# Two transformer layers: quarters of product rounds beside the scores, masked Q by DMA, V copies on GpSimd

## The chip, the cores and the metric

The kernel runs on one core of one Trainium2 chip. The core has five engines that run their own instruction streams and meet through semaphores: TensorE (PE; its weight loads are listed as PEld), VectorE (DVE), ScalarE (ACT), GpSimd (POOL) and SyncE (SP), which here only issues DMAs. The metric is the device time of one execution in microseconds.

## The reference

One sequence of 2048 rows and width 512 passes twice through an attention layer and an MLP, with the same weights both times:

```python
def _A_ref(x, wqkv, wo):                    # H = 32 heads of Dh = 16
    qkv = (x @ wqkv).reshape(B, S, 3, H, Dh).transpose(2, 0, 3, 1, 4)
    q, k, v = qkv[0], qkv[1], qkv[2]
    p = softmax(einsum("bhqd,bhkd->bhqk", q, k) * Dh ** -0.5)
    return einsum("bhqk,bhkd->bhqd", p, v).transpose(0, 2, 1, 3).reshape(B, S, D) @ wo
def _B_ref(x, w1, b1, w2, b2):              # F = 1792
    return gelu(x @ w1 + b1) @ w2 + b2
x = x + _A_ref(layernorm(x));  x = x + _B_ref(layernorm(x))
x = x + _A_ref(layernorm(x));  x = x + _B_ref(layernorm(x))
```

## The kernel before, in words

**Cells.** The attention is cut into cells. A cell is one head, one tile of 128 keys and one chunk of 512 queries: 2 layers x 32 heads x 16 key tiles x 4 chunks = 4096 cells. K and Q are stored transposed, four groups of two heads deep in the partitions: a strip `a` of 32 partitions holds two heads of 16. A *pass* takes one chunk of queries and four heads, one out of each strip, over its key tiles (16, which makes 64 cells, or fewer in the passes that are cut in two); eight passes cover the 32 heads. The last chunk of layer 1 goes in two halves of 256 queries, with both heads of a strip in one cell. To take one head of the two in a strip, the kernel makes a copy of Q, `QP`, in which the rows of the other head are zero; there are two slots of it, used by turns.

**Scores.** `score` is one matmul of 32 rows by 128 columns (the strip's 32 rows, 128 keys), which streams 512 queries into a PSUM bank. Matmuls on different strips run side by side. `scores` issues a group of two cells for ScalarE, and may add a third (`more`) or cells for VectorE (`attach`, `trade`). A run of such matmuls in one tiling is called a score stretch here. `solo` issues a VectorE cell alone.

**Exponentials.** ScalarE takes two or three cells with one Exp activation over neighbouring banks (`exps`, the profile's L2234). VectorE takes single cells (`dfirst`, L1867): one multiply-add whose integer result is read as a bfloat16, a coarse exponential. Two further copies of that tile with a constant added (`shift`, L2097, on GpSimd; or L2099 on VectorE) and products with V scaled by two weights make it precise. So a VectorE cell needs three products with V (plain V once, the scaled copies `VC` twice) where a ScalarE cell needs one. `KD` names the key tiles that may go to VectorE; `vcopies` (L1526) makes `VC`.

**Products.** `pvs` collects ready tiles into rounds: four matmuls of 128 rows (keys) by 17 columns (16 of V and a column of ones for the sum), one for each strip's head, side by side in the four column strips of one PSUM bank, number 6 (`PVB`, the only one). After the last round of a pass `norm` reads the bank.

**Rest.** Projections, output projection and the two MLP matmuls run as 128x32 tiles (`quads`, L715). Where PE would idle, `fill` lets it run matmuls whose result is not used (L1586).

**Order.** All of it is laid out before the launch by a planner (`_Plan` on `_Sched`): each job is a thread that yields operations with a cost, keys that it reads and writes, and a priority; the scheduler picks the operation that can start first by its own clock of each engine, and writes each engine's instructions in that order, with the semaphore waits that the keys demand. The engines then run their lists in order. The planner counts a change between the tilings "S" (scores) and "P" (rounds) with `SW` on PE. `ROWS` holds sets of rule values, and `PIECES` says which set holds in which part of the kernel. `_Op.apart` are matmuls issued behind an operation at no counted cost.

Of the kernel before, what the change touches and what calls it, by code (L numbers as in the profile page):

```python
# [5 lines left out]
ALU = mybir.AluOpType  # L6
# [9 lines left out]
H = 32  # L16
# [9 lines left out]
PT_RING = 30  # L26
# [37 lines left out]
KWAIT = (140, 230, 320)  # L64
KSTEP = 10
QSTEP = 10
KLAST = 1
NKD = 7
# [27 lines left out]
         "CLOSE",)  # L96
ROWS = (
# [42 lines left out]
)  # L140
PIECES = (4, 23, 28, 27, 28, 25, 25, 25, 23, 25, 20, 25, 25, 25, 20, 20, 20, 24, 15, 36, 36, 30, 31, 24, 24, 24, 33, 33, 24, 24, 24, 0, 0,
          5, 5, 37, 25, 25, 6, 25, 14, 18, 30, 30, 3, 35, 37, 5, 19, 19, 5, 20, 38, 41, 38, 35, 35, 35, 35, 24, 17, 17, 17, 14, 19, 7, 7, 7,
          18, 18, 18, 39, 39, 22, 15, 1, 41, 41, 39, 41, 39, 25, 25, 2, 2, 14, 23, 25, 25, 35, 35, 32, 32, 34, 36, 32, 38, 41, 41, 32)
# [53 lines left out]
class _Prog:  # L197
# [77 lines left out]
    def group(self, eng, fns, reads=(), writes=(), sem=None, by=1):  # L275
        if sem is None:
            sem = ENG_SEM[eng]
        self._dep_waits(eng, reads, writes)
        for i, fn in enumerate(fns):
            last = i == len(fns) - 1  # L280
            self.prog[eng].append(("do", fn, sem if last else None, by if last else 0))
# [423 lines left out]
class _Plan:  # L705
# [801 lines left out]
    def vcopies(self):  # L1507
# [4 lines left out]
        for v in range(len(first)):  # L1512
# [17 lines left out]
            if not js:  # L1530
                continue
# [890 lines left out]
```

## Time and profile before

| | |
|---|---|
| median of 3 runs | 1375.13 us (1374.58 to 1377.1) |
| profiled execution | 1374.89 us |
| its span, first to last instruction | 1373.1 us |
| granted TensorE clock | 1.0 |

The page gives busy times and groups of instructions; a group's row has its count, busy us, mean ns of one, and the idle time of its engine just before it with what ended it. Matmuls overlap and their ends are modelled, so PE's use is better read from starts in the timeline. The windows view gives busy us of each engine within a stretch, with the granted clock, the DMA engines' share and GB/s.

### The profile page before, as it was taken

The page shows a single profiled execution, that of the slowest core. Times are in us where ns is not written, and L with a number is a line of the kernel's source. Part 1 is how long each engine was busy: PE and PEld are TensorE (multiplying, and loading weights), DVE is VectorE, ACT ScalarE, POOL GpSimd, SP SyncE. Part 2 cuts the span into 40 slices and gives each one's busy share as a digit, 9 for nine tenths or more (in the row PEclk, how much of TensorE's full clock was granted, in tenths as well). Part 3 has the DMA queues.
Part 4 walks back from the last instruction along what each step waited for, and adds up shares of the span by engine and source line. Part 5 has one row for each costly group of instructions (what it writes and reads, how often), then busy time and mean ns, then how long its engine had stood idle before and what let it go on. Part 6 is the DMA issues. An engine that isn't in the chain of part 4 may idle for free.

```text
span 1373.1 us, 42332 instructions
## 1 busy us (share of the span) xinstructions
PE 1338.8 (98%) x18168; PEld 390.1 (28%) x18168; DVE 1261.8 (92%) x2504; ACT 1349.0 (98%) x1385; POOL 802.8 (58%) x1352
## 2 busy tenths in 40 slices
PE   9999999999999999999999999999999999999999
PEld 3222222222222222222222222222222222333446
DVE  8999999989999899998979899999999898999894
ACT  7999999999999999999999999999999999999995
POOL 1367667657665567665626666546656665765461
DMA  5300000123221221112451141100104314201112
GB/s 149 72 2 1 2 2 23 49 75 97 71 43 45 89 83 55 44 51 65 114 109 40 49 128 57 48 17 12 37 24 117 93 40 143 83 14 44 29 34 83
DMA packets 122296, 80.20 MB, mean 58 GB/s; under 512 B 36732, under 2 KB 121084, under 8 KB 122108
## 3 DMA queue, kind: packets, MB, share of 16 engines
q1 hardware_dynamic: 122108, 77.49, 20.6%
q8 instruction: 143, 2.34, 0.7%
q14 instruction: 45, 0.37, 0.1%
HBM read 65.67 MB, written 4.19 MB: 51 GB/s over the span
## 4 chain that ended last, share of the span: by engine, by line
ACT 83%; PE 10%; DVE 6%; DMA 1%; issue 0%
ACT pt L2234 70%; PE ps L715 5%; ACT kt L2234 3%; ACT g L1276 3%; PE ps L1598 3%; ACT v L2234 2%; PE ps L2301 2%; DVE dp L1867 2%; ACT q L2234 2%; DVE kt L1867 1%; ACT L2234 1%; ACT L1276 1%; ACT g L2234 1%; DVE stats L848 0%; DMA wr<-in_B_w_dram 0%; DMA wr<-in_A_wqkv_dram 0%
## 5 line engine op out<-in xcount | busy, mean ns | idle before, releaser
L2234 ACT ACTIVATE pt<-ps 128x1024 bf16<-128x1024 f32 (+1 forms) x1183 | 1142.7, 1176 | 2.0 <-PE ps L1598 1.6
L1598 PE MATMUL ps<-qp,kt 32*128 32x512 bf16 x4096 | 551.5, 384 | 16.6 <-ACT pt L2234 12.2
L2097 POOL INT64_ADD dp<-dp x732 | 440.2, 613 | 204.8 <-DVE dp L1867 123.1
L1867 DVE TENSOR_SCALAR dp<-ps 128x512 uint16<-128x512 f32 x733 | 483.3, 679 | 26.3 <-PE ps L1598 23.4
L1598 PEld LDWEIGHTS ps<-qp,kt 32*128 32x128 bf16 x4096 | 138.4, 91 | 569.7 <-ACT pt L2234 466.7
L2097 POOL INT64_ADD kt<-kt x320 | 190.1, 599 | 174.1 <-DVE kt L1867 93.6
L2301 PE MATMUL ps<-pt,v 128*17 128x512 bf16 (+1 forms) x2758 | 273.9, 359 | 1.4 <-ACT pt L2234 0.7
L1867 DVE TENSOR_SCALAR kt<-ps 128x512 uint16<-128x512 f32 x309 | 207.4, 683 | 23.4 <-PE ps L1598 20.8
L2301 PE MATMUL ps<-dp,vc 128*17 128x512 bf16 (+1 forms) x1652 | 220.7, 357 | 0.6 <-POOL xf L2097 0.4
L2301 PE MATMUL ps<-dp,v 128*17 128x512 bf16 (+1 forms) x826 | 139.1, 357 | 3.4 <-DVE xt L1076 2.4
L2097 POOL INT64_ADD v<-v x155 | 94.1, 611 | 71.7 <-DVE v L1867 35.8
L715 PE MATMUL ps<-xf,wr 128*32 128x512 bf16 (+1 forms) x1888 | 134.6, 366 | 0.5 <-DVE g L1258 0.4
L2301 PE MATMUL ps<-kt,vc 128*17 128x512 bf16 (+1 forms) x766 | 117.6, 340 | 1.0 <-POOL xf L2097 0.3
L1867 DVE TENSOR_SCALAR v<-ps 128x512 uint16<-128x512 f32 x154 | 102.8, 682 | 13.2 <-PE ps L1598 12.8
L715 PE MATMUL ps<-wr,g 128*32 128x512 bf16 x1408 | 108.1, 384 | 0.5 <-DVE dp L1867 0.2
L2301 PEld LDWEIGHTS ps<-pt,v 128*17 128x17 bf16 x2758 | 69.8, 88 | 74.5 <-issue 51.8
L2301 PE MATMUL ps<-kt,v 128*17 128x512 bf16 (+1 forms) x507 | 85.8, 350 | 1.7 <-DVE xt L1076 1.0
L2097 POOL INT64_ADD xf<-xf x78 | 46.5, 596 | 65.5 <-DVE xf L1867 40.3
L1258 DVE TENSOR_SCALAR g<-ps,hb1t 128x512 bf16<-128x512 f32 (+1 forms) x112 | 78.9, 706 | 1.0 <-PE ps L715 1.0
L2301 PEld LDWEIGHTS ps<-dp,vc 128*17 128x17 bf16 x1652 | 56.7, 88 | 42.0 <-issue 24.4
L2234 ACT ACTIVATE kt<-ps 128x1024 bf16<-128x1024 f32 (+1 forms) x60 | 63.4, 1189 | 0.0
L2301 PE MATMUL ps<-v,vc 128*17 128x512 bf16 x308 | 60.8, 381 | 0.0
(124 smaller groups left out, 1425.5 us busy)
## 6 DMA issues: line engine op xcount, KB each, us to landing
wr<-in_B_w_dram SPq DMA_DIRECT2D x174, 256.0 KB, 2.9
wr<-in_A_wqkv_dram SPq DMA_DIRECT2D x24, 256.0 KB, 3.3
x<-in_A_x_dram SPq DMA_DIRECT2D x7, 512.0 KB, 4.3
wr<-in_A_wo_dram SPq DMA_DIRECT2D x10, 256.0 KB, 3.7
kept<-x SPq DMA_DIRECT2D x4, 512.0 KB, 3.1
x<-kept SPq DMA_DIRECT2D x4, 512.0 KB, 4.4
out_dram<-x SPq DMA_DIRECT2D x16, 128.0 KB, 2.5
q<-in_B_w_dram SPq DMA_DIRECT2D x3, 512.0 KB, 4.5
```

Source lines behind the costliest of these rows:

```text
L715: return [lambda e, a=a: e.matmul(out[32 * a:32 * a + 32, :], lhsT=lhsT[:, 32 * a:32 * a + 32], rhs=rhs, start=start, stop=stop, tile_posi ...
L1258: yield _Op("dve", 0.21 + n / 966, lambda e, fc=fc, pb=pb: e.tensor_scalar(T["G"][:, fc, q], pb, T["HB1T"][:, fc:fc + 1], None, op0=ALU.ad ...
L1276: lambda e, g=g: e.activation(out=g, in_=g, func=ACT.Gelu_apprx_tanh), reads=gk, writes=gk, prio=2)
L1598: return (lambda e: e.matmul(o, lhsT=lhsT, rhs=rhs, start=True, stop=True, tile_position=(32 * a, 0)), ["K%d.%d.%d" % (l, gb, kt // 4), "Q ...
L1867: yield _Op("dve", 0.682, lambda e: e.tensor_scalar(u, self.bank(b), E_SCALE, E_BIAS, op0=ALU.mult, op1=ALU.add), reads=["B.%d" % b], writ ...
L2097: op = _Op("pool", PFIX + PWORD * 128 * (hi - lo), lambda e: e.int64_add(dst, src, by * PACKED), reads=reads, writes=writes)
L2234: yield _Op("act", EXPC + 0.4267 * n, lambda e, src=src, dst=dst: e.activation(out=dst, in_=src, func=ACT.Exp, scale=0.25), reads=["B.%d" ...
L2301: op.fns.append(lambda e, o=o, lhsT=q[0][0][m], rhs=q[0][1][:, n * m:n * m + n], a=a, st=st, sp=sp: e.matmul(o, lhsT=lhsT, rhs=rhs, start= ...
```

## The change

- **Quarters** (`beside`, `quarter`, `rest`, `avoid`, `freed`): behind a score stretch that leaves a strip of rows unused, PE also gets a quarter of a product round: the four products restricted to 32 of their 128 rows, as 32x32 tiles in that strip. Four quarters make a round. At most two rounds are open at a time (`PARTS`), at most one quarter goes to a stretch, a new round is opened only while each column of the pass has at least `PLEFT` (4 to 12, mostly 7) key tiles left. Each quarter waits for the one before it. What is left at the end of a pass is issued alone.
- **Wide cells** (`wide`, `solo`): a VectorE cell issued alone may run as a round of four 128-row by 32-column tiles against a copy of Q that is zero outside the head's 16 rows; only for strip 3, and only where that copy was made by DMA. `solo` gets a further condition under which it issues such a cell.
- **Masked Q** (`qpad`): instead of a multiplication by a 0/1 mask on VectorE, five DMAs copy the 16 rows of each strip's head into `QP` (the other rows stay zero) and those of strip 3 into two further slots. This holds for full-width passes that don't follow passes of four key tiles or fewer.
- **V copies** (`vcopies`, `vpart`): on GpSimd, and for the passes that are cut in parts by chunk of keys, so that a part can be used before the others.
- **Space**: `PT_RING` 29, `NKD` 6, `QP` four slots.
- **Order anew**: new rows in `ROWS`, new `PIECES`.

The core of the diff:

```diff
-PT_RING = 30
+PT_RING = 29
+PARTS = 2
+PLEFT = 7
+STEER = 1
+WSOLO = 0.4
+WBACK = 9
+QCOST = 0.6
+QTAIL = 2.2
+VCP = 1.1
-NKD = 7
+NKD = 6
...
-            for f, r, w in op.apart:
+            for f, r, w, *order in op.apart:
+                for x in order:
+                    for y in x:
+                        self.P.wait(e, *y)
                 ev = self.P.group(e, [f], r, w)
+                for x in order:
+                    x[:] = [ev]
...
+    def vpart(self, v, pi, js):
...
+            yield _Op("pool", 0.2 + VCP * len(js) / 6, lambda e, i=i, w=w: e.tensor_scalar(
+                T["VC"][:, v % VCR, i, js[0]:js[-1] + 1, 0:H // 4 * 17], src, w, None, op0=ALU.mult),
...
-            s = yield ("acq", "qp")
+            s = pi % 2
+            yield ("take", ("qp", s))
+            if len(ts) == 1 and ts[0] == s and pi > 1 and min(len(x[3]) for x in self.pas[pi - 2:pi]) > 4:
+                fns = []
+                for a in range(4):
+                    p = slice(32 * a + DH * s, 32 * a + DH * s + DH)
+                    fns.append(lambda e, ...: e.dma_start(T["QP"][p, s, :], T["Q"][p, b, 512 * qc:512 * qc + 512]))
+                p = slice(96 + DH * s, 96 + DH * s + DH)
+                fns.append(lambda e, ...: e.dma_start(T["QP"][p, 2 + s, :], T["Q"][p, b, 512 * qc:512 * qc + 512]))
+                yield _Op("sp", QCOST, fns, ..., sem="dqp%d" % s, by=80, tail=QTAIL)
...
+    def beside(self, op, start, cells):
+        if self.s.mode != "S":
+            self.laid = False
+        cur = self.cur
+        if cur is None or self.laid or not all(cur["begun"]):
+            return
+        idle = [r for r in range(4) if all(c[2] != r for c in cells)]
+        if not idle:
+            return
+        cur["more"] = min(self.pvleft[k] for k in cur["cols"]) >= PLEFT
+        part = next((x for x in cur["parts"] if x["left"] & set(idle)), None)
+        if part is None and cur["more"] and len(cur["parts"]) < PARTS:
...
+        r = next(r for r in idle if r in part["left"])
+        part["left"].discard(r)
+        op.apart.append((self.quarter(cur, part, r, ...), part["keys"], ["B.%d" % cur["b"]], self.order))
+        self.laid = True
...
+    def quarter(self, cur, part, r, end):
+        bank, n = self.bank(cur["b"]), cur["n"]
+        row = slice(32 * r, 32 * r + 32)
+        def f(e):
+            for m in range(512 // n):
+                for a, ws, p in part["work"]:
+                    x = e.matmul(bank[32 * a:32 * a + 17, n * m:n * m + n], lhsT=ws[m][row, :], rhs=p[row, n * m:n * m + n],
+                                 start=False, stop=..., tile_position=(32 * r, 32 * a))
+            return x
+        return f
...
+    def wide(self, cell, qs, bank):
...
+        return (self.quads(self.bank(bank), self.T["K"][l][:, gb, kt * 128:(kt + 1) * 128], self.T["QP"][:, 2 + qs, :], True, True),
+                ["K%d.%d.%d" % (l, gb, kt // 4), "QZ.%d" % qs])
...
+            cur["more"] = False
+            yield ("cond", lambda cur=cur: not cur["parts"] or self.ended or self.s.force or self.s.clock["act"] < self.s.clock["pe"] + 0.3)
+            self.cur = None
+            for i, x in enumerate(cur["parts"]):
+                self.s.force = False
+                for r in sorted(x["left"]):
+                    op = _Op("pe", MM, [self.quarter(...)], reads=x["keys"], writes=["B.%d" % b], prio=0.5, mode="S")
+                    op.late = lambda op, start: self.P.wait("pe", "pe", self.P.cnt["pe"])
+                    yield op
```

More of the change, by code (lines that the diff above doesn't have):

```diff
@@ L64 @@
 KWAIT = (140, 230, 320)
+PARTS = 2
+PLEFT = 7
+PAGE = 10
+STEER = 1
+WSOLO = 0.4
+WBACK = 9
+WSIDE = 0
+QCOST = 0.6
+QTAIL = 2.2
+VCP = 1.1
 KSTEP = 10
@@ L1529, in vcopies @@
-            yield ("give", ("vc", v))
-            if not js:
-                continue
-            self.lend = 1
+            if not kd:
+                continue
+            old = used[v % VCR]
+            if old is not None:
+                yield ("cond", lambda pi=first[old + 1]: self.pv >= pi)
+                for part in self.vparts(first[old]):
+                    yield ("need", ("vc", old, part[-1]))
+            used[v % VCR] = v
+            for part in self.vparts(first[v]):
+                yield ("spawn", self.vpart(v, first[v], part), 4)
@@ L1561, in free @@
         k = "B.%d" % PVB
-        if best[1] > now and (self.pvwas if k in ahead else self.pvopen) and "VC.0.0" in P.lastw:
+        if best[1] > now and (self.pvwas if k in ahead else self.pvopen) and "VC.0.0.0" in P.lastw:
             best = (PVB, 0.0)
@@ L1599, in score, with avoid @@
                 ["K%d.%d.%d" % (l, gb, kt // 4), "QP.%d" % qs] + ["K0.0.0.b"] * ((l, gb) == (0, 0) and kt in (2, 3)))
+    def avoid(self):
+        parts = self.cur["parts"] if self.cur and STEER else []
+        left = set.union(*[x["left"] for x in parts]) if parts else set()
+        return left if parts and (len(parts) == PARTS or not self.cur["more"]) and len(left) < 3 else set()
     def next_act(self, used=()):
+        most = self.avoid() | set(used)
         while self.pa < len(self.pas):
@@ L1604, in next_act @@
                 if q:
-                    return q.pop(next((k for k, c in enumerate(q) if c[2] not in used), 0))
+                    k = next((k for k, c in enumerate(q) if c[2] not in most), None)
+                    return q.pop(next((k for k, c in enumerate(q) if c[2] not in used), 0) if k is None else k)
             self.pa += 1
         return None
-    def next_d(self, used, start, pop=True):
+    def beside(self, op, start, cells):
[10 more added lines that the diff above has]
+        if part is None and cur["more"] and len(cur["parts"]) < PARTS:
+            got = []
+            for k in cur["cols"]:
+                for q in (self.aq[k], self.dq[k]):
+                    i = next((i for i, x in enumerate(q) if ("V", cur["l"], x[5], x[5] // 4) in self.s.tokens and self.s.landed(x[2]) <= start
+                              and not any(y[0] == "seen" for y in x[3])), None)
+                    if i is not None:
+                        got.append((k, q, i))
+                        break
+            if len(got) < 4 or cur["wait"] and not self.rest(got, start):
+                return
+            part = {"left": set(range(4)), "work": [], "keys": [], "back": []}
+            for k, q, i in got:
+                x = q.pop(i)
+                part["work"].append((k[1], x[0], x[1]))
+                part["keys"] += x[2]
+                part["back"] += x[3]
+                self.pvleft[k] -= x[4]
+            cur["parts"].append(part)
+        if part is None:
+            return
+        r = next(r for r in idle if r in part["left"])
+        part["left"].discard(r)
+        op.apart.append((self.quarter(cur, part, r, len(cur["parts"]) == 1 and not part["left"] and not any(self.pvleft[k] for k in cur["cols"])),
+                         part["keys"], ["B.%d" % cur["b"]], self.order))
+        self.laid = True
+        self.units_done += 1
+        if not part["left"]:
+            cur["parts"].remove(part)
+            for pool, x in self.freed(part["back"]):
+                self.s.pools[self.s.route(pool, x)].append(x)
@@ new lines, in rest @@
+    def rest(self, got, start):
+        took = [id(q[i]) for _, q, i in got]
+        for k in self.cur["cols"]:
+            for q in (self.aq[k], self.dq[k]):
+                x = next((x for x in q if id(x) not in took), None)
+                if x is not None and ("V", self.cur["l"], x[5], x[5] // 4) in self.s.tokens and self.s.landed(x[2]) <= start:
+                    return True
+        return False
+    def quarter(self, cur, part, r, end):
[4 more added lines that the diff above has]
+                for a, ws, p in part["work"]:
+                    x = e.matmul(bank[32 * a:32 * a + 17, n * m:n * m + n], lhsT=ws[m][row, :], rhs=p[row, n * m:n * m + n], start=False, stop=end and m == 512 // n - 1,
+                                 tile_position=(32 * r, 32 * a))
+            return x
+        return f
@@ new lines, in freed, with next_d @@
+    def freed(self, back):
+        for pool, r in back:
+            if pool == "seen":
+                r[0]["seen"][r[1]] += 1
+                continue
+            if pool == "du":
+                self.duleft[r] -= 1
+                if self.duleft[r]:
+                    continue
+            if pool == "pl":
+                if not self.drop(*r):
+                    continue
+                r = r[1]
+            yield pool, r
+    def next_d(self, used, start, pop=True, wide=False):
@@ L1650, in join @@
             self.open = None
-        f, r = self.score(d, self.s.tokens[("qp", d[0])], b)
+        f, r = (self.wide if op.mode == "P" else self.score)(d, self.s.tokens[("qp", d[0])], b)
         if op.fns and not self.third(b):
@@ L1656, in join @@
         else:
-            op.fns.append(f)
+            op.fns += f if op.mode == "P" else [f]
             op.reads += r
@@ L1881, in chance @@
                 return self.ended
+            bank = bool(pools["dbank"] or pools["misc"]) and bool(self.open or self.roomy())
+            if bank and s.clock["dve"] <= s.clock["pe"] + WSOLO and s.clock["act"] >= s.clock["pe"] + WBACK:
+                side = sum(th.op.cost for th in s.threads if th.op is not None and th.op.eng == "pe" and th.prio >= 10)
+                if side <= WSIDE and self.next_d((), s.clock["pe"], False, True):
+                    return True
             if s.clock["act"] < s.clock["pe"] + ALONE:
@@ L1893, in solo @@
                 return
-            d = self.next_d((), s.clock["pe"])
+            d = self.next_d((), s.clock["pe"], wide=True)
+            mode = "P" if d else "S"
+            self.wides += mode == "P"
+            d = d or self.next_d((), s.clock["pe"])
             b = (pools["dbank"] or pools["misc"]).pop(0)
-            op = _Op("pe", MM, [], mode="S", prio=1.2)
+            op = _Op("pe", MM, [], mode=mode, prio=1.2)
             extra = []
             self.join(op, d, b, extra)
+            if mode == "S":
+                op.late = lambda op, start, d=d: self.beside(op, start, [d])
             yield op
@@ L2259, in pvs @@
             begun = [False] * 4
+            self.cur = cur = {"b": b, "l": l, "n": n, "cols": cols, "begun": begun, "parts": [], "more": True, "wait": False}
             def have(k):
@@ L2294, in build @@
                     rounds += 1
-                    end = all(self.pvleft[k] == sum(q[0][4] for x, q in got if x == k) for k in cols)
+                    end = not cur["parts"] and all(self.pvleft[k] == sum(q[0][4] for x, q in got if x == k) for k in cols)
                     for m in range(512 // n):
```

96 lines of the change are left out of this document (56 added, 40 removed), and 122 rows, old and new, of the table ROWS.

## The prediction

> **What bounds the kernel now.** I read the page first, then the windows, then a stretch of the timeline in the middle, then groups by line.
>
> ```profile
> span 1373.1 us, 42332 instructions
> PE 1338.8 (98%) x18168; PEld 390.1 (28%) x18168; DVE 1261.8 (92%) x2504; ACT 1349.0 (98%) x1385; POOL 802.8 (58%) x1352
> ACT 83%; PE 10%; DVE 6%; DMA 1%; issue 0%
> ```
> The last line is the chain that ended last: mostly ScalarE's exponentials (L2234). The profiled run took 1374.89 us, 1.8 over its span and 0.24 below the median of the three runs shown, 1375.13; I sum against the span and add 1.8. About 0.2% (2.75 us) is what a measurement can tell from no change.
>
> ```profile
> 13.80:1360.00 1346.20, 1317.13 (x17802) 378.52 (x17806) 1249.42 (x2453) 1338.29 (x1363) 799.89 (x1343) 1.00 0.21 57
> 300.00:400.00 100.00, 99.02 (x1256) 26.22 (x1252) 98.25 (x208) 100.00 (x109) 64.56 (x108) 1.00 0.32 78
> 700.00:800.00 100.00, 97.75 (x1262) 25.65 (x1262) 85.23 (x144) 99.94 (x101) 54.33 (x91) 1.00 0.23 61
> ...
>   PE ps L1598: 63.1, 172
> ```
> Busy us of PE, PEld, DVE, ACT, POOL, then granted clock, DMA share, GB/s. Between the first score and the last layer's end (1346.2 us; 26.9 lie around it) ScalarE idles 7.9 us. Nothing shortens that part unless cells (one score tile of 128 keys by 512 queries) leave ScalarE for VectorE. VectorE is 92.8% busy there, 98% in some stretches and 85% in others; 63.1 us of its idle time before L1867 ends with a score from PE (last line). So three engines stand close together, and a relief must reach all three.
>
> ```profile
> 600.38 0.39 PE L1598 MATMUL ps<-qp,kt 32*128 32x512 bf16 x3
> 600.70 0.40 PE L715 MATMUL ps<-xf,wr 128*32 128x512 bf16 x4
> 600.92 0.39 PE L2301 MATMUL ps<-v,vc 128*17 128x512 bf16 x3
> 601.25 0.39 PE L1598 MATMUL ps<-qp,kt 32*128 32x512 bf16 x3
> 601.57 0.39 PE L2301 MATMUL ps<-pt,v 128*17 128x512 bf16 x1
> 601.58 0.38 PE L2301 MATMUL ps<-v 128*17 128x512 bf16 x1
> ```
> Starts tell PE's true price (ends are modelled). Round to round is 0.22 us; score to round 0.32, round to score 0.33: each change of tiling costs 0.10, and a stretch of scores with both changes 0.43. The four matmuls of a round start within 0.01. The stretches hold three cells: one of four 32-row strips streams nothing.
>
> ```profile
> L2234 ACT ACTIVATE pt<-ps x1183: 1017/1177/1682, 12.2 to 1339.9; 128x1024 bf16<-128x1024 f32 x180, 128x1536 bf16<-128x1536 f32 x18
> L2234 ACT ACTIVATE kt<-ps x60: 1017/1177/1647, 212.1 to 809.7; 128x1024 bf16<-128x1024 f32 x56, 128x1536 bf16<-128x1536 f32 x4
> L2234 ACT ACTIVATE v<-ps x46: 1030/1182/1627, 1003.5 to 1343.8; 128x1024 bf16<-128x1024 f32 x39, 128x1536 bf16<-128x1536 f32 x7
> L2234 ACT ACTIVATE q<-ps x26: 1055/1190/1641, 215.4 to 1178.9; 128x1024 bf16<-128x1024 f32 x23, 128x1536 bf16<-128x1536 f32 x3
> L2234 ACT ACTIVATE g<-ps x8: 1024/1476/1637, 342.6 to 878.9; 128x1536 bf16<-128x1536 f32 x5, 128x1024 bf16<-128x1024 f32 x3
> 1108.48 3.67 ACT q L2234 x4
> L1867 DVE TENSOR_SCALAR dp<-ps x733: 628/680/1137, 37.7 to 1339.8; 128x512 uint16<-128x512 f32 x184
> L1867 DVE TENSOR_SCALAR kt<-ps x309: 627/683/693, 140.0 to 1330.6; 128x512 uint16<-128x512 f32 x155
> L1867 DVE TENSOR_SCALAR v<-ps x154: 645/681/693, 197.9 to 658.3; 128x512 uint16<-128x512 f32 x154
> L1867 DVE TENSOR_SCALAR xf<-ps x77: 652/682/693, 31.7 to 1185.0; 128x512 uint16<-128x512 f32 x77
> L1867 DVE TENSOR_SCALAR xp<-ps x54: 628/680/692, 33.5 to 765.8; 128x512 uint16<-128x512 f32 x54
> ```
> 1323 exponentials, so some 1323 score stretches. The chain spends 3.67 on four of two cells: 0.46 per cell. VectorE has 1327 of the 4096 cells, at 0.68 each.
>
> **1. Quarters in the idle strip.** A round of four 128-row products is cut into four 32-row quarters, each issued behind a score stretch in a strip that it leaves free, at most one per stretch. 4096 cells are 64 passes of 64 cells, with 20.7 stretches each. A new round may start while all columns have 7 of 16 key tiles left, over 9/16 of a pass (11.6); the first products must be begun, and the two rounds open at the end run on: I take 12 per pass, 770 quarters. If they stream beside the scores, each saves a quarter of 0.22 (0.055) and costs four more starts (0.01): 35 us of PE. Upper end: 1300 quarters at 0.055, 71 us. The lower end is below zero, since no row shows 32-column beside 128-column tiles. The nearest:
>
> ```profile
> 1356.28 0.33 PE L902 MATMUL ps<-ident,xln 128*128 128x128 bf16 x3
> 1356.55 0.40 PE L715 MATMUL ps<-q,g 128*32 128x512 bf16 x4
> L902 PE MATMUL ps<-ident,xln x24: 219/219/230, 8.1 to 1356.4; 128*128 128x128 bf16 x24
> ```
> Three transposes in 0.33 with 0.22 each step by 0.055; the third has streamed at 1356.45, and the 128x32 tiles start at 1356.55. Going from 128 to 32 columns alone thus costs 0.10, on shared rows. Against that, score cells on different strips start together. I take the strips as independent, nearest to that row, which is the only one with disjoint rows; the other reading is rival D. By the Trainium skill, TensorEngine Tiling (Array Packing), Key Properties, a change of tiling mode drains the array, and 32x128 and 32x32 are listed as two modes; by that rule each quarter costs two drains and the sum is D's. The trace agrees for shared rows (0.10); no run here shows disjoint ones.
>
> A quarter's buffers stay held for up to four stretches, and PE waits for its own previous quarter: done one round earlier (0.33+0.32 ahead), so nothing. Behind that wait stands all of PE.
>
> **2. Masked Q by DMA; V copies on GpSimd.**
>
> ```profile
> L1545 DVE TENSOR_SCALAR qp<-q,mask 128x512 bf16<-128x512 bf16 x75 | 25.4, 338 | 0.2 <-PE ps L1598 0.2
> L1526 DVE TENSOR_SCALAR vc<-v 128x816 bf16<-128x816 bf16 x60 | 21.1, 357 | 0.0
> L1526 DVE TENSOR_SCALAR vc<-v 128x680 bf16<-128x680 bf16 x10 | 3.4, 370 | 0.0
> L1526 DVE TENSOR_SCALAR vc<-v 128x136 bf16<-128x136 bf16 x18 | 2.9, 188 | 0.0
> L1196 SPq DMA_DIRECT2D wr<-in_B_w_dram x174: 367/368/955, 10.7 to 1348.6; - x174
> x<-in_A_x_dram SPq DMA_DIRECT2D x4, 128.0 KB, 2.3
> SPq L1196 <- PE ps L1598: 535.0, 86, 152.2
> L2097 POOL INT64_ADD dp<-dp x732 | 440.2, 613 | 204.8 <-DVE dp L1867 123.1 <-DVE ott L1085 14.6 <-DVE qp L1545 13.2
> L756 POOL MEMSET v<- 128x512 bf16 x1 | 2.3, 2275 | 0.0
> ```
> Of the 75 full-width masks, 9 follow the first short passes and 11 the short ones of layer 1; 55 go to DMA: 18.6 us off VectorE, and the copies another 27.4: 46.0.
>
> SP pays 55 x 5 issues of 0.37: 1.8 us each, landing 1.8 + 2.3 = 4.1 us after the first (nearest row: 128 KB loads; 2.7 if the issues overlap, 13.4 if all five landings queue up). Hidden, by either bound: a mask's slot frees when the pass two before has been scored, 21 us (1346.2/64) ahead of its use. Not hidden: SP works in order, and its weight loads wait for ring buffers up to 152.2 us; a mask behind such a load is late, and every score of its pass with it. That is rival E; here zero. The mask's wait on SP in turn holds the weight loads behind it, whose ring is four deep: zero.
>
> GpSimd takes 88 copies of up to 816 elements. Its rows give bounds: an add of 0.61 and a memset of 2.28; far apart and neither a copy, so I take their geometric mean, 1.2: 106 us (54 to 200). By the Trainium skill, GPSIMD Engine Reference, Elementwise side-by-side cycle accounting, a light one-input body runs at 1.03 cycles per element, as an estimate 0.70 us at 1.2 GHz for 816 elements, so 62 us; the trace shows no such copy. Behind a pair of copies an add waits 2.4 us, and product rounds behind that. GpSimd goes from 800 us to 800 + 106 + 38 (31 more pairs of cells, two adds of 0.61 each) = 944 of 1318, 72%, and its idle 28% and the other products that PE can take first hide that: zero, and at most 44 x 2.4 = 106 us if nothing did. The zeroing of the extra Q rows, one memset at the start while GpSimd idles: zero. One exponential buffer fewer of 30: no ScalarE wait of the trace ends with PE's products, zero; without that cover it costs ScalarE waits of a round, 0.22.
>
> **3. Lone cells as rounds.** A lone cell costs a stretch of 0.43 now; as 32-column tiles of all 128 rows it costs a round, 0.22. Only strip 3 with a DMA-made mask qualifies, and the new condition for extra ones needs ScalarE 9 us ahead, as around its GELUs. 0 to 100 cells, 0 to 21 us of PE; I take 5.
>
> **4. How much moves (order anew).** Let x cells leave ScalarE and M be the length of the middle. ScalarE: M = 1346.2 - 0.46x. VectorE, busy a share s: 1249.4 - 46.0 + 0.68x = sM. If nothing but its load changes, s = 92.8%, x = 41, M = 1327. If all its waits for scores went, s = 97.5% (63.1/1346.2 more); the best windows have 98%, which gives x = 102, M = 1299. PE decides between them.
>
> ```profile
> L1586 PE MATMUL ps<-b2row 128*32 128x512 bf16 x324 | 26.9, 384 | 0.1
> L1586 PE MATMUL ps<-b2row,zero 128*17 128x512 bf16 x80 | 7.3, 383 | 0.0
> ```
> 101 rounds are fillers, 22 us; without them PE is busy 1295 of 1346.2, 96.2%. With the change: -35 quarters, -5 lone cells; and per moved cell -0.21 (half a stretch), +0.11 (two more products of four to a round), and 1.5 seats, as the cell and half of the one that its stretch carried need one: 0 in a fourth strip, 0.43 alone, 0.21 taken: +0.32. Together 1255 + 0.215x. At the old 96.2% that meets ScalarE's line at x = 61, M = 1318; VectorE then stands at s = 94.5%, between its bounds. Sum: span 1318 + 26.9 = 1345, time **1347** (28 us less, 2.0%). Ends, by s: 1328 (98%) and 1356 (92.8%).
>
> **Rivals.** B, the change does not do what it says: quarters are rare, or eat their gain in held buffers and in left-over quarters that end a pass alone (0.43 each, with a wait for the one before). With no net gain from them PE needs 1290 + 0.215x, which meets ScalarE at x = 8, M = 1343: time 1371. For it: VectorE and PE were both short of slack, so little else moves. Against: an idle strip in almost every stretch. Range 1356 to 1371.
>
> D, slower: the strips are not independent, and a quarter drains the array, as the 0.10 for 128 to 32 columns suggests. Then it streams behind the scores, 0.22 + 0.10 more, in place of 0.055 saved: 770 x 0.32 = 246 us on PE, 1290 + 246 + 13 = 1549 at x = 61, nearly full: about 1590. It decides early: once a quarter adds over 0.01 us net, PE needs 8 us more than in B and the whole is slower than before. Against it: four scores on different strips start within 0.01 and need no common timing.
>
> E, slower: masks late on SP. Scores of a pass then wait with all engines; 0.5 to 1 us in each of 55 passes makes 28 to 55 us: 1375 to 1402. For it: the 535 us of SP waits. Against: 21 us of lead.
>
> **How the numbers follow.** The forecast (1328 to 1356) 0.56, B 0.17, no change (within 0.2%: 1372.4 to 1377.9) 0.06, E 0.07, D 0.14. Faster 0.73, same 0.06, slower 0.21. The range leaves out D and the forecast's lowest edge: 1326 to 1400, where most lies below 1372; the forecast's own range is 1328 to 1356.
>
> **What would show it.** Quarters right: matmuls of 32 rows by 17 columns start within 0.02 us after the scores, and score to next round stays near 0.32; wrong (D): 0.64 there, VectorE and ScalarE idle on PE. Their number near 770. Masks: a DMA into the Q copy with some 4 us to landing and no score waiting for it; otherwise E. L1545 at 20 full-width rows, no V copy on VectorE; GpSimd copies near 1.2 us, busy 72%. L1867 near 1390 operations, exponentials near 1290, ScalarE busy down 28 us with its middle still 99% full; if ScalarE's middle has holes, PE or VectorE ends the steps and the sum is wrong even where the time is right. GpSimd waits that end on its own copies would show my zero there to be wrong.

## The result, and the profile after

With the change the kernel takes 1.71 times as long: 2367.43 us (median of four runs, 2331.83 to 2395.6) against 1375.14 for the kernel before, a ratio of 1.7057 with a 95% interval of 1.6877 to 1.7237. The ratio takes the two faster of the four runs alone (2331.83 and 2360.56 us, clock 0.785 and 0.771), since the other two (0.753 and 0.765) are in a slower state, over 1.5% above the fastest. The prediction said 1347 us, with 1326 to 1400 as its range. The profiled execution is the one of 2395.6 us.

The page of the kernel after: span, busy time by engine, granted TensorE clock in 40 slices (tenths of full speed), and the chain that ended last.

```profile
span 2393.8 us, 48982 instructions
PE 1898.6 (79%) x21251; PEld 471.6 (20%) x21251; DVE 1301.2 (54%) x2377; ACT 1426.2 (60%) x1380; POOL 990.3 (41%) x1492
PEclk9768888677875767788768776765689887565688
PE 61%; issue 20%; POOL 10%; DVE 5%; ACT 3%; DMA 0%; POOLq 0%
```

Before, three engines were over 90% busy and ScalarE carried 83% of the chain. Now no engine is full, the chain runs through PE and "issue" (time in which an engine waits for nothing that the profile shows), and the clock has fallen, on average to 0.75 in this execution. Two places show where it goes. First the GpSimd queue: what the view by source lists for L1602, the V copies, and, of L2290, the adds, their configuration instructions (min/median/max ns), then a stretch of its timeline, where square brackets hold the idle time before an operation and what ended it.

```profile
L1602 POOL TENSOR_SCALAR vc<-v x122: 549/1565/2292, 29.8 to 2329.0; 128x816 bf16<-128x816 bf16 x52, 128x136 bf16<-128x136 bf16 x30, 128x272 bf16<-128x272 bf16 x30, 128x544 bf16<-128x544 bf16 x10
L1602 POOLq MODIFY_POOL_CONFIG  x92: 1/11/14, 7.7 to 2319.8; - x92
```

```profile
L2290 POOLq MODIFY_POOL_CONFIG  x92: 4/11/12, 32.5 to 2331.5; - x92
```

```profile
1182.00 3.84 POOL L1602 TENSOR_SCALAR vc<-v 128x272 bf16<-128x272 bf16 x4 [7.46 <-issue]
1191.61 0.98 POOL L2290 INT64_ADD kt<-kt  x2 [5.77 <-issue]
1192.58 3.69 POOL L2290 INT64_ADD dp<-dp  x6
```

Each time GpSimd goes from adds to copies it stands still for some 7 us, and for nearly 6 us on the way back, with two MODIFY_POOL_CONFIG at each; 92 of them each way make 46 round trips (median pauses 7.2 and 5.9 us). Who pays is in the waits (us in total, times, longest us):

```profile
DVE dp L2050 <- PE ps L1686: 616.7, 377, 14.5
PEld ps L2495 <- POOL kt L2290: 186.5, 43, 14.9
PE ps L2495 <- POOL kt L2290: 171.1, 18, 14.6
```

The longest waits of these rows, 14.5 to 14.9 us, have the length of one trip there and back with its copies. In the stretch shown PE stood for 11.4 us, until the add at 1191.61 was done: PE waits for an add, and VectorE and ScalarE then wait for scores. Second, PE's own stream, here in a stretch at half clock (start, length, operation):

```profile
599.40 0.61 PE L1686 MATMUL ps<-qp,kt 32*128 32x512 bf16 x3
599.94 0.60 PE L1763 MATMUL ps<-pt,v 32*17 32x512 bf16 x4
600.48 0.60 PE L2495 MATMUL ps<-v,vc 128*17 128x512 bf16 x2
```

L1763 is a quarter. It starts 0.54 us after the scores, not with them, and the round 0.54 after it. At full clock, elsewhere in the same trace, both steps are 0.32. That is rival D's picture.

### The profile page after: what moved, and what is told of

Its sections match the earlier page's. It is cut to its first block, busy times and chain, and to the rows that moved or that the text cites. A ratio compares the mean times of both kernels' runs of the same rounds, so it can differ in the third digit from the quotient of the medians.

```text
span 2393.8 us, 48982 instructions
## 1 busy us (share of the span) xinstructions
PE 1898.6 (79%) x21251; PEld 471.6 (20%) x21251; DVE 1301.2 (54%) x2377; ACT 1426.2 (60%) x1380; POOL 990.3 (41%) x1492
## 4 chain that ended last, share of the span: by engine, by line
PE 61%; issue 20%; POOL 10%; DVE 5%; ACT 3%; DMA 0%; POOLq 0%
PE ps L2495 17%; PE ps L1686 17%; PE ps L772 16%; PE ps L1763 11%; POOL vc L1602 6%; ACT pt L2427 3%; POOL dp L2290 2%; DVE dp L2050 1%; POOL kt L2290 1%; PE ps L1674 1%; DVE kt L2050 1%; DVE xp L2050 0%; POOL xf L2290 0%; DVE v L2050 0%; POOL v L2290 0%
## 5 line engine op out<-in xcount | busy, mean ns | idle before, releaser
L2427 ACT ACTIVATE pt<-ps 128x1024 bf16<-128x1024 f32 (+1 forms) x1245 | 1267.4, 1066 | 886.3 <-PE ps L1686 642.9
L2050 DVE TENSOR_SCALAR dp<-ps 128x512 uint16<-128x512 f32 x798 | 538.8, 686 | 627.7 <-PE ps L1686 616.7
L2290 POOL INT64_ADD dp<-dp x795 | 476.5, 610 | 390.2 <-DVE dp L2050 171.1
L1686 PE MATMUL ps<-qp,kt 32*128 32x512 bf16 x3997 | 627.4, 453 | 8.0 <-ACT pt L2427 5.2
L2495 PE MATMUL ps<-dp,vc 128*17 128x512 bf16 (+1 forms) x1786 | 314.4, 435 | 135.8 <-POOL kt L2290 51.3
L1763 PE MATMUL ps<-pt,v 32*17 32x512 bf16 (+1 forms) x3184 | 349.0, 426 | 1.6
L1602 POOL TENSOR_SCALAR vc<-v 128x816 bf16<-128x816 bf16 (+3 forms) x122 | 177.8, 1458 | 354.6 <-issue 233.5
L2495 PE MATMUL ps<-pt,v 128*17 128x512 bf16 (+1 forms) x2094 | 312.4, 433 | 10.6 <-POOL kt L2290 9.5
L2290 POOL INT64_ADD kt<-kt x296 | 175.5, 597 | 340.2 <-DVE kt L2050 156.8
L2495 PE MATMUL ps<-dp,v 128*17 128x512 bf16 (+1 forms) x894 | 191.0, 428 | 83.6 <-POOL dp L2290 40.1
L2495 PE MATMUL ps<-kt,vc 128*17 128x512 bf16 (+1 forms) x725 | 156.8, 421 | 92.7 <-POOL kt L2290 58.6
L2290 POOL INT64_ADD v<-v x143 | 86.6, 608 | 149.2 <-DVE v L2050 72.5
L1763 PEld LDWEIGHTS ps<-pt,v 32*17 32x17 bf16 x3184 | 71.1, 84 | 210.7 <-PE ps L2495 97.6
```

The lines of the kernel that those rows point to most:

```text
L1602: yield _Op("pool", 0.2 + VCP * len(js) / 6, lambda e, i=i, w=w: e.tensor_scalar(T["VC"][:, v % VCR, i, js[0]:js[-1] + 1, 0:H // 4 * 17], ...
L1686: return (lambda e: e.matmul(o, lhsT=lhsT, rhs=rhs, start=True, stop=True, tile_position=(32 * a, 0)), ["K%d.%d.%d" % (l, gb, kt // 4), "Q ...
L1763: x = e.matmul(bank[32 * a:32 * a + 17, n * m:n * m + n], lhsT=ws[m][row, :], rhs=p[row, n * m:n * m + n], start=False, stop=end and m == ...
L2050: yield _Op("dve", 0.682, lambda e: e.tensor_scalar(u, self.bank(b), E_SCALE, E_BIAS, op0=ALU.mult, op1=ALU.add), reads=["B.%d" % b], writ ...
L2290: op = _Op("pool", PFIX + PWORD * 128 * (hi - lo), lambda e: e.int64_add(dst, src, by * PACKED), reads=reads, writes=writes)
L2427: yield _Op("act", EXPC + 0.4267 * n, lambda e, src=src, dst=dst: e.activation(out=dst, in_=src, func=ACT.Exp, scale=0.25), reads=["B.%d" ...
```

## The experiments

**Which parts cost it.** Three runs undo the GpSimd copies (e1), the quarters (e2, by `PARTS`) and both (e3). The planner lays each one's order anew.

```diff
e1: -  yield _Op("pool", 0.2 + VCP * len(js) / 6, ..., mode="V")
    +  yield _Op("dve", VFIX + VPER * len(js), ...)
e2: -PARTS = 2
    +PARTS = 0
e3: both
```

> The changed kernel with the V copies back on VectorE; the planner lays the order out anew from the same rules. Theory R (GpSimd reloads its code at each change between V copies and integer adds: the trace of the changed kernel shows 92 pairs of configuration instructions, 7.3 us before a copy and 5.9 us before the add after it): most of the loss goes. Theory Q (each quarter is a stretch of its own, since its 32-column tiles wait until the 128-column ones have drained): 746 quarters at 0.32 us instead of 0.055 saved remain, some 200 us, so 1560 to 1620 us if the granted clock stays 1, up to 1800 if it falls. If Q alone made the loss, it stays above 2200 us.

> The changed kernel without quarters (no round is ever opened beside the scores), V copies still on GpSimd. R: 46 visits with some 19 us each (13.2 us of reloading and about 6 us of copies) in which the integer adds and so the products of VectorE's cells stand still: 1375 + 46 x 14 to 46 x 19 = 2000 to 2250 us, with a granted clock well under 1. Q alone: 1375 to 1450 us, clock 1.

> V copies on VectorE and no quarters: masks by DMA, wide cells, smaller rings and the new rules are left. R and Q together: the loss is gone, 1365 to 1400 us, clock 1. If the masks by DMA come late for the scores (rival E of the prediction) 1400 to 1450 us, with scores that wait for a DMA.

Measured: e1 1633.39 us (ratio 1.1878, 1.1829 to 1.1928), e2 2017.16 (1.4669, 1.4622 to 1.4717), e3 1423.51 (1.0352, 1.0322 to 1.0382). e2 lies in its range, e1 13 us above the one for a full clock. Busy times of the three, in this order, the first two with the clock:

```profile
PE 1586.9 (97%) x21423; PEld 462.9 (28%) x21423; DVE 1287.1 (79%) x2468; ACT 1421.8 (87%) x1388; POOL 798.1 (49%) x1353
PEclk9999999999999999999999969999999999999999
```

```profile
PE 1472.2 (73%) x18635; PEld 409.9 (20%) x18635; DVE 1254.3 (62%) x2350; ACT 1379.9 (68%) x1381; POOL 962.4 (48%) x1452
PEclk9788788998888888898788889675798888868879
```

```profile
PE 1359.1 (96%) x18567; PEld 398.5 (28%) x18567; DVE 1248.7 (88%) x2451; ACT 1367.9 (96%) x1384; POOL 789.7 (56%) x1338
```

Counted from e3, the quarters alone cost 210 us (e1), the GpSimd copies alone 594 (e2), both 923 (the two runs of after that the ratio takes). The 119 that are neither's go in part with the clock: the records hold full and half clock, so a mean of 0.845 in e2 is some 625 of its 2018 us at half clock, and 0.771 to 0.785 in those two runs some 1000 to 1080 us, and there a quarter's steps are 0.54 in place of 0.32. Added up over the traces, the steps from scores to their quarters are 296 us in after and 241 in e1, 55 more; what makes the rest of the 119 is not shown. The clock goes with the holes in PE's work: it is 0.98 or more in the runs whose PE is 95 to 98% busy (before, e1 and e3 among them) and 0.75 to 0.85 where the copies leave PE 72 to 79% busy (after, e2, and e5 below). What e3 keeps, 48 us over before, missed its expectation and is taken up below.

**What a quarter and a copy cost by themselves.** A kernel of its own, whose output is its input: none of the layers is computed. PE runs blocks of 60 turns of scores and a round (A), scores, quarter, round (B), the same with each 32x128 score tile cut into four 32x32 tiles (C), cut scores and a round (D), four scores and a round (E), quarter and round (F); GpSimd runs adds, copies of 816 elements, and both by turns.

> Not the layers: TensorE alone runs 60 times each of A three score tiles of 32x128 and a round; B the same with a quarter (four 32x17 tiles) in the free strip between; C as B with each score tile cut into four of 32x32; D as A with the scores so cut; E four score tiles and a round; F a quarter and a round. GpSimd alone runs integer adds, scaled copies of 816 elements, the two by turns, adds and memsets by turns, copies and memsets by turns. The output is the input. Q: A and E 0.64 us per turn, B 0.96; C as D and near A (about 0.68), since all its tiles have one size. If a quarter cost only its own starts, B would be 0.66. R: adds alone 0.61, copies alone 1.6, by turns some 13 us more per pair; memsets without a reload beside either.

Measured, us per turn: A 0.653, B 0.973, C 0.690, D 0.680, E 0.657, F 0.650. PE's timeline in B, then in C (L50 scores, L54 32-row tiles, L59 rounds):

```profile
63.28 0.39 PE L50 MATMUL ps<-x 32*128 32x512 bf16 x3
63.60 0.39 PE L54 MATMUL ps<-x 32*17 32x512 bf16 x4
63.92 0.40 PE L59 MATMUL ps<-x 128*32 128x512 bf16 x4
...
121.68 0.43 PE L54 MATMUL ps<-x 32*32 32x512 bf16 x16
122.04 0.40 PE L59 MATMUL ps<-x 128*32 128x512 bf16 x4
```

A quarter behind 128-column scores adds 0.320 (B less A), though it has a strip to itself and waits for no data. Once the scores have 32 columns too, it adds 0.010 (C less D), what the prediction had taken. So here a change of the tile's size keeps matmuls apart, and strips of their own don't let them overlap. But cutting the scores costs 0.027 (D less A), which leaves 0.055 less 0.037, 0.018 us, as the gain of a quarter. GpSimd's timeline in the same run:

```profile
8.20 6.98 POOL L98 INT64_ADD u<-u  x10 [7.77 <-DVEq L30]
22.14 23.26 POOL L101 TENSOR_SCALAR wb<-vb 128x816 bf16<-128x816 bf16 x10 [6.95 <-issue]
51.24 0.60 POOL L98 INT64_ADD u<-u  x1 [5.84 <-issue]
58.71 2.29 POOL L101 TENSOR_SCALAR wb<-vb 128x816 bf16<-128x816 bf16 x1 [6.87 <-issue]
66.94 0.60 POOL L98 INT64_ADD u<-u  x1 [5.95 <-issue]
```

```profile
L104 POOL MEMSET wb<- 128x816 bf16 x20 | 15.5, 777 | 1.2
```

The pause of 6.9 and 5.9 us needs no other engine and comes at every turn; a single copy between adds costs 15.1 us (2.29 + 6.87 + 5.95). The copy itself takes 2.25 (1.6 was expected), against an add's 0.61. Memsets by turns with adds and with copies (last row: 0.777 each, 1.2 us of idle time before all 20) show no pause.

**The copies alone, in the kernel before.** Its V copies go to GpSimd whole, and no rule of the change comes with them; the planner lays the order anew.

```diff
-  yield _Op("dve", VFIX + VPER * len(js), ...)
+  yield _Op("pool", 0.2 + 1.1 * len(js) / 6, ..., mode="V")
```

> The kernel before, with one edit: its 70 scaled V copies (two to each of some 33 visits) go to GpSimd, whose other work is shifts and adds. Theory R (each change of GpSimd between an add and a copy costs a pause): the second run less the third gave 594 us for 46 such changes there and back, 12.9 each; with 33 to 40 of them 430 to 520 us come to 1375, so 1750 to 1900 us, GpSimd idle for 7 us before a copy and 6 before the next add, and PE waiting for adds. Rival N (the pauses cost so much only in the new order, where the copies are cut in 122 parts): GpSimd has 42% free, the pauses lie in that, and the time stays below 1450.

Measured: 2008.65 us, ratio 1.4615 (1.4589 to 1.4641).

```profile
L1526 POOLq MODIFY_POOL_CONFIG  x88: 1/11/17, 5.8 to 1929.4; - x88
```

Worse than expected, in the direction of theory R: there are 92 copies and not 70, 88 MODIFY_POOL_CONFIG make 44 trips and not 33 to 40, and 633 us over them is 14.4 us each, not 12.9. The copies themselves take 172 us in all, far less than the loss. Neither the change's rules nor the cutting in parts is needed for it.

**The quarter repaired.** e1's kernel with scores cut into 32x32 tiles wherever a quarter follows.

```diff
+  def cut(e):
+      for c in range(4):
+          x = e.matmul(o[32*c:32*c+32, :], lhsT=lhsT[:, 32*c:32*c+32], rhs=rhs, ..., tile_position=(32*a, 32*c))
+      return x
```

> The first experiment (V copies on VectorE, the rest as after) with one edit: in every stretch of scores that takes a quarter, each 32x128 score tile is issued as four tiles of 32x32, so that quarter and scores are of one size. Theory T (a change of tile size drains PE, strips apart or not): 0.32 us a quarter goes and the cut costs 0.027 a stretch and the quarter 0.010 (fourth run), so the 852 quarters cost some 32 us in place of 273: 1633 less 241 is 1390, or, with the four 0.055 us of each round that a quarter saves set against it, the third run's 1423 less 13 is 1410; 1385 to 1425. Rival B (the quarter waits for its bank, its buffers or the quarter before it): nothing goes, 1620 to 1660 or more.

Measured: 1437.23 us, ratio 1.0457 (1.0422 to 1.0492); 196 us of e1's loss are gone, though the time is 12 us above the range. Its timeline (L1693 cut scores, L1773 the quarter):

```profile
601.81 0.41 PE L1693 MATMUL ps<-qp,kt 32*32 32x512 bf16 x8
601.83 0.39 PE L1773 MATMUL ps<-pt,v 32*17 32x512 bf16 x4
602.15 0.39 PE L2505 MATMUL ps<-dp,vc 128*17 128x512 bf16 x2
```

The quarter now starts 0.02 after the scores and the round 0.32 after it: same data, banks and waits as in e1, another tile size. That settles it for theory T against rival B. A stretch of three cut cells with its quarter takes 0.36 in place of 0.32 (e4, C and A). Still it is 14 us slower than e3, which has no quarters, where 13 faster was expected: the 0.018 that each should save does not reach the end. Why is open; the orders of e3 and e8 differ. It is not quarters left over and issued alone, as in the prediction's rival B: 844 of the 852 stand behind scores, and their steps from scores to quarter add up to 3 us where e1 has 241.

**What is left in e3.** The same code with the order's settings of before (`ROWS`, `PIECES`), no lone-cell rounds, with the masked Q by DMA (e6) and by VectorE (e7).

> After's code without quarters and 128-row rounds of lone cells, V copies on VectorE, the order's settings those of before: of the change only the masked Q by DMA and the new planning rules are left. Theory M (what is left in the third run, 48 us over before, comes mostly from the masked Q's DMAs: SP waits for a row to come free, and the weights' loads queue behind it): 1400 to 1420 us, and at least 20 us of PE idle time that ends with a weights DMA (32.8 in the third run, 1.2 in before). Rival W (the 128-row rounds of lone cells cost it) and rival O (the new settings of the order cost it): 1372 to 1385 us, with PE hardly waiting for weights.

> The run before this one with the masked Q made by VectorE again: of the change only the planning rules and the slightly smaller rings of buffers are left. Theory M: 1372 to 1385 us, PE idle before weights under 5 us. If the rules or the smaller rings cost what is left in the third run: 1400 to 1425 us, with the same waits as in the run before.

Measured: e6 1406.86 (ratio 1.0230, 1.0211 to 1.0250), e7 1392.88 (1.0132, 1.0115 to 1.0149). e6 is in theory M's range, e7 in none. Both theories get a part: 14 us go with the DMAs, 18 were there without them. PE's idle time before matmuls that read weights, by what ended it, in before, e3, e6, e7:

```profile
  DMA wr<-in_B_w_dram: 1.2, 4
```

```profile
  DMA wr<-in_B_w_dram: 32.8, 31
```

```profile
  DMA wr<-in_B_w_dram: 16.0, 23
```

```profile
  DMA wr<-in_B_w_dram: 5.4, 11
```

Theory M had asked for at least 20 us of it in e6, where there are 16.0.

e7 has the old settings, no DMA for masks, no quarter and no GpSimd copy. It differs from before mainly in one row of `PT_RING` and in V copies cut in 122 parts (92 before). Each by itself: e9 is the kernel before with one number changed, e10 is e7 with 30 rows again and the Q ring at its old size (shown by its first line).

```diff
e9:  -PT_RING = 30
     +PT_RING = 29
e10: -PT_RING = 29
     +PT_RING = 30
     ...
```

> The kernel before with one number changed: PT_RING, the rows that hold weights between an exponential and its rounds, 29 in place of 30 (the change gives that row to the zero-padded Q). Theory P (the missing row, or any other small disturbance of the order that the settings were chosen for, is what the run with the rules alone lost, 18 us): 1388 to 1396 us, with more of VectorE's idle time before scores than before's 63.1. Rival V (the V copies cut in 122 parts cost it): 1374 to 1380.

> The run with the rules alone (1392.9 us), with PT_RING 30 again and the Q ring at its old size; the V copies stay in 122 parts on VectorE. Theory P in its narrow form (the row): 1374 to 1380. In its wide form (any disturbance of the order), and by rival V: 1386 to 1396.

Measured: e9 1392.36 (1.0122, 1.0107 to 1.0137), e10 1389.37 (1.0107, 1.0090 to 1.0124). Either alone costs 14 to 17 us and both together 18. They don't add, which speaks for theory P in its wide form: what costs is less the row or the parts than that the order is laid anew with settings chosen for another kernel. It is not shown apart from them, since each edit lays the order anew; e12 below tests it from the other side. In e9 VectorE stood idle before scores for 95.0 us in 245 places (63.1 in 172 before):

```profile
  PE ps L1598: 95.0, 245
```

e11 adds lone cells' rounds to e6 (`d = self.next_d((), s.clock["pe"], wide=True)` and the further condition in `solo` restored). e12 is e11 with 63 of the 100 numbers in `PIECES` chosen anew by the planner's own costs.

> The run with masked Q by DMA alone (1406.9 us), with the 128-row rounds of lone cells added, still with the order's settings of before. The third run, which has the new settings too, took 1423.5. If the lone cells' rounds cost the 17 us between them: 1418 to 1428. If the new settings do: 1400 to 1411. By the prediction's step on lone cells (5 us of PE saved): 1400 to 1404.

> The run before this one on the list (masked Q by DMA, 128-row rounds of lone cells, V copies on VectorE, no quarters; 1416.4 us) with 63 of the 100 numbers in PIECES chosen anew, by the costs of the kernel's own planner. Theory P (what a disturbance of the order costs is the misfit of the settings to the new plan): some 13 to 17 us come back, 1398 to 1405 us. If the loss is in what the plan doesn't see (weights behind the masks' DMAs on SP, smaller buffers): 1411 to 1421. At or below before's 1375 if the relief of VectorE was worth something that the settings hid.

Measured: e11 1416.38 (1.0305, 1.0278 to 1.0332), e12 1395.27 (1.0145, 1.0128 to 1.0162). e11 missed its ranges: the lone cells' rounds come with 9.5 us more and the new settings with the other 7. New settings alone bring back 21 us, more than expected, which bears theory P out. With so much misfit, runs whose order was laid anew can price neither the DMAs nor VectorE's relief. Two more runs keep before's order, instruction for instruction on PE, VectorE, ScalarE and GpSimd: e13 adds the 55 groups of five DMAs on SP, into a buffer in DRAM that nobody reads; e14 shortens VectorE's masks and V copies.

```diff
e13: +  fns.append(lambda e, ...: e.dma_start(spare[p, s, i // 4, :], T["Q"][p, b, 512 * qc:512 * qc + 512]))
     +  op.late = lambda op, start: [self.P.wait("sp", *ev) for ev in free]
e14: -  T["QP"][:, s, w * i:w * i + w], q, ...
     +  T["QP"][:, s, w * i:w * i + (16 if pi > 8 else w)], q[:, 0:16 if pi > 8 else w], ...
```

> The kernel before with its order left as it is, instruction for instruction, and the change's 55 groups of five DMAs of masked Q added on SP, each behind the same wait (until PE has read the row's old scores), but into a spare buffer that nobody reads: VectorE still makes the masked Q. Theory M (the DMAs hold SP's queue and the weights come late behind them): 1385 to 1392, the 14 us between the runs with and without them, with over 10 us of PE idle time before weights (2.2 in before). Theory P (those 14 us were the order's misfit): 1374 to 1378, under 5 us before weights.

> The kernel before with its order left as it is, and VectorE's masks (after the first nine passes) and scaled V copies (after the first eight visits) cut to 16 and 17 columns: the rest of those rows keeps old values, so this part of the computation is left out. VectorE does some 35 us less. If VectorE's time is worth anything in itself, as the prediction had it (46 us off VectorE make room for 61 cells): 1355 to 1368. If the order written ahead decides (which engine takes a cell is fixed when the order is laid): 1371 to 1376, with VectorE's idle time before scores up by about what is saved.

Measured: e13 1385.06 (1.0076, 1.0062 to 1.0090), e14 1374.39 (0.9996, 0.9987 to 1.0005). In e13, PE's idle time before weights, and SP's longest waits at the masks' DMAs (L1561) and at the weights' (L1200):

```profile
  DMA wr<-in_B_w_dram: 19.1, 26
```

```profile
SPq L1200 <- PE ps L1614: 300.0, 89, 40.6
SPq L1561 <- PE ps L1614: 190.5, 29, 16.1
```

Theory M holds, at the low edge of its range: what SP issues behind a mask waits with it, and there are 19.1 us of PE idle time for 1.2 before (the 2.2 of the expectation counts another row of weights), and 10 us at the end. Whether SP's waits at the masks or their issues (0.42 us, the median of the 275) weigh more is not separated. The two groups on VectorE in before and in e14, and in e14 its idle time before scores:

```profile
L1545 DVE TENSOR_SCALAR qp<-q,mask 128x512 bf16<-128x512 bf16 (+1 forms) x91 | 29.8, 327 | 0.2 <-PE ps L1598 0.2
L1526 DVE TENSOR_SCALAR vc<-v 128x816 bf16<-128x816 bf16 (+4 forms) x92 | 28.6, 322 | 0.1
```

```profile
L1546 DVE TENSOR_SCALAR qp<-q,mask 128x16 bf16<-128x16 bf16 (+1 forms) x91 | 20.7, 227 | 0.2 <-PE ps L1599 0.2
L1526 DVE TENSOR_SCALAR vc<-v 128x17 bf16<-128x17 bf16 (+2 forms) x92 | 15.7, 184 | 0.1
```

```profile
  PE ps L1599: 70.2, 199
```

They fell from 29.8 and 28.6 us to 36.4 in all, 22 us (35 were expected: an instruction of 16 columns still takes 0.2), VectorE's busy time as a whole by 14 (1261.8 to 1247.8), its idle time before scores rose by 7, and the time did not move. With the order fixed, relief of VectorE of this size is worth nothing; the 46 us of the prediction were not tried.

## Why the prediction was wrong, point by point

**Quarters, "strips taken as independent".** Failed. The number of quarters was good (3456 matmuls of L1763 and its like, 864 quarters, for 770), the premise wasn't. Rival D, priced there at 0.32 a quarter and 246 us, is what happened: 0.320 in e4, and 210 us in the kernel (e1 less e3), where the 852 quarters of e1 at 0.320 less the 0.055 that each takes from a round would make 226. e1, which has the quarters and not the copies, took 1633 us for D's about 1590; the range had left D out. The nearest row in the trace, the step of 0.10 between tiles of 128 and 32 columns, had said so. So had the rule cited there from the Trainium skill, TensorEngine Tiling (Array Packing), Key Properties, that a change of mode drains the array. e4's B and C (0.320 against 0.010) now agree with it for disjoint rows. The argument against it, scores on four strips starting together, compared tiles of one size.

**V copies on GpSimd, "zero".** Failed, by far the most. The term was 1.2 us a copy (2.25 measured for 816 elements) and at most 106 us in all; what counted, a pause of 13 us for each trip, was in no row of before and not in the bounds. The prediction did have product rounds wait behind an add that waits for a pair of copies, but for 2.4 us, and it let GpSimd's 28% of idle time hide that; with the pauses such a wait is up to 14.9 us, and nothing hid it: 594 us (e2 less e3) and 633 (e5). GpSimd's busy time, 990 us for 944 predicted, is nearly right all the same, by luck: the pauses are idle time, and do not show in it. The Trainium skill has a load of this kind: GPSIMD Engine Reference, Instruction dispatch, says that the first call to a freshly loaded kernel (a routine of GpSimd) pays a load of some 6 us, seen as a gap behind MODIFY_POOL_CONFIG. e4's trace agrees in size (6.7 to 7.3 us one way, 5.7 to 6.1 the other), and shows a pause at each change, in both directions. The prediction cited only the cost of elements from that page of the Trainium skill (an estimate of 0.70 us a copy), where e4 measured 2.25.

**The granted clock.** The sum took 1.0 throughout. In these runs it stayed at 0.98 or more where PE was 95 to 98% busy; in after, with holes of up to 14.9 us, it fell to between 0.753 and 0.785, which also made each quarter dearer (0.54 a step for 0.32).

**Masked Q by DMA.** Nearly right for the masks themselves, wrong behind them. Hardly a score waited for one (e3's waits have 2.2 us of PE before scores that end with a mask's DMA), so rival E, late scores, fell; the DMAs were 275 as counted, landing 1.8 us after their issue, which took 0.59 each (median) and not 0.37. But "holds the weight loads behind it: zero" cost 10 us (e13).

**Lone cells.** 99 in after (396 matmuls, four to a round), at the top of the 0 to 100 and not some 24, which 5 us stood for; and no gain shows: e11 is 9.5 us over e6, though misfit of the order is in that difference.

**How much moves.** Failed as a method. 1318 exponentials in after and 1323 before; VectorE has 1347 cells in after, not 1390. Without quarters and GpSimd copies the relief moved nothing either: VectorE has 1302 cells in e3, 1327 before. Which engine takes a cell is fixed when the order is laid; free time on VectorE then lengthened its waits and left the time as it was (e14). The steps of the sum on rates ("span 1345") supposed an order that adapts, while one number that makes it be laid anew costs 17 us (e9).

Open are the 14 us between e8 and e3, lone cells at a fixed order, which wasn't tried, and the rest of the 119 us that quarters and copies cost only together.

## What to carry to other kernels

Before moving work to another engine, ask what else that engine runs: an operation of 2.25 us alone cost a pause of 13 us here each time the kind changed and changed back, and the queue behind it paid. Matmuls on disjoint strips overlapped in these runs when their tile sizes agreed and not when they differed; a premise with no row behind it deserves a small kernel of its own first. In an order written ahead, price a part with the order held fixed (add or shorten the instructions alone), for laying it anew moved the time by 14 to 17 us here, more than the masks' DMAs cost.

## What the runs showed of the hardware that was not expected

- In e4 GpSimd stands still for 6.7 to 7.3 us when it goes from integer adds to scaled copies and for 5.7 to 6.1 us on the way back, each time; memsets of 0.777 among the adds cost no such pause.
- On PE, 32x32 tiles in a free strip start 0.02 to 0.04 us after 32x32 tiles in others (e8), but 0.32 us after 32x128 tiles (e4, B).
- A fourth score tile of 32 rows costs 0.004 us on top of three (E less A), and a score tile cut in four some 0.009 (D less A, three tiles).
- 275 DMAs of 16 KB on SP, at 0.42 us of issue each (median), cost 10 us in e13, where PE waited 19.1 us for weights in place of 1.2, although nothing waited for the DMAs' own data.
